# Gated mix of linear attention and a spatial-shift MLP on one core: q tails turned, attention accumulated in w4's banks, VectorE work evened, one early turn and the loads of x, w1 and w2 re-ordered

## The chip, the cores and the metric

The kernel runs on one core of one Trainium2 chip. The metric is the time of one execution on the device, in microseconds; with one core, the slowest core is that core. Each run is put down with its granted TensorE clock and a state: fast, or slow where it lies more than 1.5% above the fastest run of the same kernel. Before the change the median was 259.9 us in 3 runs (259.82 to 260.29).

## The reference

Sequence 2048, width 640, 32 heads of 20, one batch, bf16 inputs. Two blocks read the same x and are mixed by a per-token gate.

```python
def _A_ref(x, wqkv, wo):                       # linear attention
    q, k, v = split_heads(x @ wqkv)            # H = 32, Dh = 20
    phi = lambda t: jnp.where(t > 0, t + 1, jnp.exp(t)) + 1e-6
    pq, pk = phi(q), phi(k)
    kv = einsum("bhsd,bhse->bhde", pk, v)
    z = einsum("bhsd->bhd", pk)
    o = einsum("bhqd,bhde->bhqe", pq, kv) / (einsum("bhqd,bhd->bhq", pq, z)[..., None] + 1e-6)
    return merge_heads(o) @ wo

def _B_ref(x, w1, w2, w3, w4):                 # spatial-shift MLP
    h = _gelu(_layernorm(x) @ w1)
    hs = shift_four_quarters_along_tokens(h) @ w2
    x1 = x + hs
    return x1 + _gelu(_layernorm(x1) @ w3) @ w4     # w3: 640x1728, w4: 1728x640

g = _sigmoid((x * gate_w).sum(-1, keepdims=True))
return g * _A_ref(...) + (1 - g) * _B_ref(...)
```

## The kernel before

The sequence is 16 tiles of 128 tokens, in 4 chunks of 512. A list of work items with dependencies is put in order when the kernel is built, so TensorE's instruction order is fixed. The stages on TensorE are: warm-up, q and k of all tiles with x turned by DMA (to about 53 us); products of phi(k) with x, which stand in for kv because v is never formed (to about 70 us); w1 and w2 (to about 134 us); then w3, attention and w4 mixed together, chunk by chunk, to the end. `phi` is one ScalarE exp and two VectorE operations. TensorE accumulates in 8 banks of 512 fp32 columns; a "held" bank is kept out of the rotation until its owner is done.

The loads of x and of the weights, in the order in which they are issued:

```python
    load_x(4)
    x_turn(3)                                  # a transposing DMA on the SP queue, x_tok -> xT
    # ... gate weights ...
    for c in range(1, NCH):                    # one load for each chunk, then its four turns
        t0 = 5 if c == 1 else 4 * c
        dma_in(x_tok[:, t0:4 * c + 4, :], x2[128 * t0:512 * (c + 1), :].rearrange(...), "xc%d" % c)
        for t in range(4 * c, 4 * c + 4):
            x_turn(t)

    def load_w1():                             # on GpSimd's software queue
        dp = [k_done[5]]
        ...
    def load_w2():
        dp = [k_done[8]]
        ...
```

q of a tile: 5 matmuls of 512 columns and 5 of 128 (the "tail", output columns 512 to 639). The first three tiles are streamed by weight slice, in a hand-written order, where `(2, None)` is the turn of x tile 2 on TensorE and `(t, k)` is slice k of tile t:

```python
    def q_tile(t):
        tok = slice(128 * t, 128 * (t + 1))
        b = pair()
        mm_group(ps[:, b, 0:512], [(xT[:, k, tok], wq[:, k, 0:512]) for k in range(KD)])
        mm_group(ps[:, b + 1, 0:128], [(xT[:, k, tok], wq[:, k, 512:D]) for k in range(KD)])
        phi(b, pq_tok[:, t + 1, :])

    def q_three():
        order = [(0, 0), (1, None), (0, 1), (1, 0), (1, 1), (0, 2), (1, 2), (2, None), (0, 3), (1, 3), (0, 4), (2, 0),
                 (2, 1), (1, 4), (2, 2), (2, 3), (2, 4)]
        stream(order, wq, 128, lambda t, b: phi(b, pq_tok[:, t + 1, :]))
```

Attention of a tile, and its sum into an SBUF accumulator `abx` that already holds (1 - g) * x1. Later w4's result is scaled and added to it:

```python
    def a_tile(t):
        ...
        ts(pool, abx[:, sa, :], x_tok[:, t, :], stg[:, 3, t:t + 1], 0.0, ALU.mult, ALU.add)
        b = pair()
        mm_group(ps[:, b, 0:512], [(pqnT[:, j, tok], M_sb[:, j, 0:512]) for j in range(KD)])
        mm_group(ps[:, b + 1, 0:128], [(pqnT[:, j, tok], M_sb[:, j, 512:D]) for j in range(KD)])
        stt(abx[:, sa, :], psf[:, 512 * b:512 * b + D], stg[:, 2, t:t + 1], abx[:, sa, :], ALU.mult, ALU.add)

    def w4_half(t):                            # first matmuls of a chunk's w4: takes its six banks
        b0, b2, bt = pair(), pair(), pair()
        ...
        bank_hold.update((b0, b0 + 1, b2, b2 + 1, bt, bt + 1))

    def w4_tile(t):
        ...                                    # 13 matmuls, start=False
        for o, n0, n1 in parts:
            stt(x_tok[:, t, n0:n1], o, stg[:, 3, t:t + 1], abx[:, sa, n0:n1], ALU.mult, ALU.add)
```

## Time and profile before

| | before |
|---|---|
| median | 259.9 us (3 runs; 260.04 with three more in the comparison below) |
| span of the profiled run, granted clock | 258.4 us, 1.00 |
| TensorE matmuls, busy | 1600, 255.2 us (99%) |
| start of the first k matmul | 9.91 us |
| start of the first kv product / first attention matmul / last matmul | 53.46 / 138.34 / 256.15 us |

The page of the kernel before, parts 1 (busy time of each engine) and 4 (the chain of work that ended last, by engine):

```profile
PE 255.2 (99%) x1600; PEld 130.5 (51%) x1600; DVE 151.3 (59%) x290; ACT 109.6 (42%) x223; POOL 93.9 (36%) x152
PE 96%; DMA 2%; SPq 0%; DVE 0%; issue 0%
```

TensorE is busy all the time and the chain is nothing but TensorE after the first few microseconds. Such a kernel can be sped up only by fewer or cheaper matmuls, by an earlier start, or by a shorter end after the last matmul (2.29 us here). A busy TensorE is not proof that it issues at its fastest, so the starts of successive matmuls were compared as well: 215.8 ns apart for 512 columns, 109.2 for 256 and 55.8 for 128. The Trainium skill ("TensorE: Matmul & The Clock Gate", the section "Wait — 56ns, not 53.3ns?") gives N / 2.4 GHz plus about 2.5 ns for a warm array. That is 215.8, 109.2 and 55.8 ns, so this trace agrees, and each narrow matmul that is merged away saves 2.5 ns.

The timeline of TensorE at the start of the kernel before (start, duration, engine, source line, operation, and in brackets the idle time before it and what ended it):

```profile
6.74 0.22 PE L899 MATMUL ps<-wq,xT 128*128 128x128 bf16 x1
7.15 0.45 PE L614 MATMUL ps<-ident,x_tok 128*128 128x128 bf16 x5 [0.19 <-DMA x_tok<-in_A_x_dram]
...
9.91 0.38 PE L898 MATMUL ps<-wkg,xT 128*128 128x512 bf16 x1
```

The second line is the turn of x tile 2. It waited 0.19 us for the tile's load, and it is TensorE's last wait for anything but itself.

### The profile page before, as it was taken

The numbers are of one execution on the slowest core, as the hardware profiler recorded it, in microseconds if no ns is written. First come the engines' busy times: TensorE is split into PE (matmuls) and PEld (weight loads), VectorE is DVE, ScalarE is ACT, GpSimd is POOL, SyncE is SP. The second block draws the span as 40 slices with busy tenths as digits, with TensorE's granted clock in tenths as the row PEclk, the third lists the DMA queues.
The fourth block names the chain that finished last, engine by engine and source line by source line (L and its number), as shares of the span: only waits on it lengthen the run. The fifth ranks groups of instructions, "written<-read, shape, count | busy, mean of one in ns | idle before, by whom it ended". The sixth has DMA issues, their size and how long they took to land.

```text
span 258.4 us, 4134 instructions
## 1 busy us (share of the span) xinstructions
PE 255.2 (99%) x1600; PEld 130.5 (51%) x1600; DVE 151.3 (59%) x290; ACT 109.6 (42%) x223; POOL 93.9 (36%) x152
## 2 busy tenths in 40 slices
PE   8999999999999999999999999999999999999996
PEld 3555555544454554555444555444465444644453
DVE  2587877899914999999993403995004410044333
ACT  1496677751366866676854240005510045300000
POOL 5013995969952118767903202222002110012001
PEclk9999999999999999999999999999999999999999
DMA  6764999682764898562825651115010020010211
GB/s 217 215 154 136 208 183 137 178 131 51 100 128 80 152 405 258 65 103 51 105 59 115 123 70 20 28 25 152 0 23 0 0 101 3 0 20 3 103 51 51
DMA packets 54307, 25.86 MB, mean 100 GB/s; under 512 B 45668, under 2 KB 52877, under 8 KB 54288
## 3 DMA queue, kind: packets, MB, share of 16 engines
q1 hardware_dynamic: 52112, 21.21, 37.4%
q0 software_dynamic: 1168, 3.28, 5.7%
q10 hardware_dynamic: 1008, 1.11, 1.2%
q8 instruction: 12, 0.20, 0.3%
q14 instruction: 7, 0.06, 0.1%
HBM read 12.04 MB, written 2.62 MB: 57 GB/s over the span
## 4 chain that ended last, share of the span: by engine, by line
PE 96%; DMA 2%; SPq 0%; DVE 0%; issue 0%
PE ps L603 61%; PE ps L1209 18%; PE ps L805 8%; PE ps L1188 3%; DMA x_tok<-in_A_x_dram 2%; PE ps L898 2%; PE ps L1096 1%; PE ps L1168 1%; SPq L285 0%; PE ps L899 0%; DVE x_tok L642 0%; PE ps L977 0%; PE ps L1006 0%; PE ps L614 0%; PE ps L1172 0%
## 5 line engine op out<-in xcount | busy, mean ns | idle before, releaser
L603 PE MATMUL ps<-xnT,w 128*128 128x512 bf16 x360 | 81.3, 380 | 0.0
L659 ACT ACTIVATE h2T<-ps 128x512 bf16<-128x512 f32 x52 | 30.5, 598 | 60.4 <-PE ps L603 60.4
L603 PEld LDWEIGHTS ps<-xnT,w 128*128 128x128 bf16 x360 | 34.2, 98 | 38.3 <-issue 0.3
L625 POOL TENSOR_SCALAR abx<-x_tok,stg 128x640 f32<-128x640 bf16 x16 | 14.8, 925 | 99.7 <-DVE x_tok L642 94.6
L1209 PE MATMUL ps<-w,h2T 128*128 128x512 bf16 (+1 forms) x260 | 50.1, 348 | 0.0
L642 DVE SCALAR_TENSOR_TENSOR x_tok<-ps,stg,abx 128x512 bf16<-128x512 f32 (+1 forms) x20 | 13.3, 670 | 62.0 <-PE ps L1209 62.0
L625 POOL TENSOR_SCALAR xn<-x_tok,st 128x640 bf16<-128x640 bf16 x32 | 35.3, 1110 | 17.8 <-DMA xnT<-xn 17.3
L1209 PEld LDWEIGHTS ps<-w,h2T 128*128 128x128 bf16 x260 | 22.9, 98 | 22.1 <-issue 0.3
L659 ACT ACTIVATE Er<-ps 128x640 bf16<-128x640 f32 x32 | 22.5, 708 | 15.0 <-PE ps L603 8.0
L658 ACT ACTIVATE junk<-x_tok 128x640 bf16<-128x640 bf16 x32 | 23.6, 739 | 3.4 <-DVE x_tok L640 2.8
L603 PE MATMUL ps<-M_sb,pqnT 128*128 128x512 bf16 (+1 forms) x160 | 24.4, 300 | 0.0
L659 ACT ACTIVATE hsT<-ps 128x512 bf16<-128x512 f32 (+1 forms) x32 | 19.0, 593 | 12.1 <-PE ps L603 11.6
L603 PE MATMUL ps<-w,hsT 128*128 128x512 bf16 (+1 forms) x160 | 23.7, 300 | 0.0
L642 DVE SCALAR_TENSOR_TENSOR abx<-ps,stg,abx 128x640 f32<-128x640 f32 x16 | 14.1, 883 | 15.8 <-PE ps L603 8.8
L603 PE MATMUL ps<-wkg,xT 128*128 128x130 bf16 (+1 forms) x140 | 21.4, 299 | 0.0
L603 PEld LDWEIGHTS ps<-M_sb,pqnT 128*128 128x128 bf16 x160 | 13.6, 98 | 13.0
L603 PE MATMUL ps<-wq,xT 128*128 128x512 bf16 (+1 forms) x130 | 19.8, 300 | 0.0
L603 PEld LDWEIGHTS ps<-w,hsT 128*128 128x128 bf16 x160 | 13.3, 98 | 12.3
L805 PE MATMUL ps<-pk_tok,x_tok 128*128 128x512 bf16 x80 | 17.8, 380 | 0.0
L625 DVE TENSOR_SCALAR Er<-Er 128x640 bf16<-128x640 bf16 x32 | 11.6, 363 | 8.1 <-ACT Er L659 8.0
L1125 DVE TENSOR_TENSOR pq_tok<-pq_tok,dnr 128x300 bf16<-128x300 bf16 (+1 forms) x48 | 15.7, 381 | 0.6
L640 DVE SCALAR_TENSOR_TENSOR x_tok<-ps,x_tok 128x640 bf16<-128x640 f32 x16 | 13.1, 820 | 4.5 <-PE ps L603 3.8
(84 smaller groups left out, 250.6 us busy)
## 6 DMA issues: line engine op xcount, KB each, us to landing
w<-in_B_w_dram SPq DMA_DIRECT2D x1, 2160.0 KB, 8.3
w<-in_B_w_dram SPq DMA_DIRECT2D x1, 2080.0 KB, 13.9
out_dram<-x_tok SPq DMA_DIRECT2D x3, 640.0 KB, 3.1
x_tok<-in_A_x_dram SPq DMA_DIRECT2D x2, 640.0 KB, 5.0
w<-in_B_w_dram POOLq DMA_DIRECT2D x8, 160.0 KB, 4.5
x_tok<-in_A_x_dram SPq DMA_DIRECT2D x5, 160.0 KB, 4.9
wv<-in_A_wqkv_dram POOLq DMA_DIRECT2D x1, 800.0 KB, 6.7
wq<-in_A_wqkv_dram ACTq DMA_DIRECT2D x4, 160.0 KB, 4.1
```

The source lines that it names most:

```text
L603: ins = e.matmul(out_ap, l, r, start=(i == 0), stop=(i == n - 1))
L625: return engf(lambda e: e.tensor_scalar(out_ap, in_ap, s1, s2, op0, op1), rd, [out_ap], cost=cost)
L640: return dve(lambda e: e.scalar_tensor_tensor(out_ap, in0, scalar, in1, op0, op1, accum_out=accum), rd, [out_ap, accum], cost=cost + 70.0)
L642: return dve(lambda e: e.scalar_tensor_tensor(out_ap, in0, scalar, in1, op0, op1), rd, [out_ap], cost=cost)
L658: return act(lambda e: e.activation(out_ap, in_ap, func, bias=bias, scale=scale, accum_out=accum), rd, wr, cost=cost)
L659: return act(lambda e: e.activation(out_ap, in_ap, func, bias=bias, scale=scale), rd, wr, cost=cost)
L805: ins = e.matmul(o, l, r, start=(t0 + q_ == 0), stop=(t0 + q_ == NT - 1))
L898: e.matmul(ps[:, b, 0:512], l, w[:, k, 0:512], start=(k == 0), stop=(k == KD - 1))
L1096: ins = e.matmul(o, l, r, start=st, stop=sp)
L1125: dve(lambda e, o=o, i0=i0, i1=i1: e.tensor_tensor(o, i0, i1, ALU.mult), [i0, dnr[:, 1, sd, :]], [o], cost=cost)
L1188: ins = e.matmul(o, l, r, start=False, stop=(i == KFF - 1))
L1209: ins = e.matmul(o, l, r, start=False, stop=(i == KFF - 1), skip_group_check=(n0 > 0))
```

## The change

Its intent has four parts.

1. **q tails turned.** For tiles 4 to 15 the tails of a chunk's four tiles become one group: the weight slice is the stationary side and 512 tokens stream past. 20 matmuls of 128 columns become 5 of 512. The result is [feature, token], so phi writes it to `mT` and a transposing DMA puts it back.
2. **Attention in w4's banks.** Attention is no longer summed into `abx` by VectorE. Its matmuls open the very banks in which w4 goes on accumulating. For that the attention weights are scaled by g / (1 - g) beforehand, so that the final multiplication by (1 - g) suits both; the gate is made with exp instead of tanh. In chunks 0 to 2 the tails are turned as well (20 narrow matmuls become 10 of 256 columns). In return six banks are held from the attention on, which leaves two for w3.
3. **x tile 2 turned one step later** in the hand-written order.
4. **Loads.** x tiles 8 to 15 come in one load, and w1 and w2 are loaded two and one key tiles later.

The diff, cut to its core:

```diff
-    for c in range(1, NCH):
-        t0 = 5 if c == 1 else 4 * c
-        dma_in(x_tok[:, t0:4 * c + 4, :], ...)
-        for t in range(4 * c, 4 * c + 4):
+    for t0, t1 in ((5, 8), (8, NT)):
+        dma_in(x_tok[:, t0:t1, :], ...)
+        for t in range(4 if t0 == 5 else t0, t1):
             x_turn(t)
     def load_w1():
-        dp = [k_done[5]]
+        dp = [k_done[7]]
     def load_w2():
-        dp = [k_done[8]]
+        dp = [k_done[9]]
@@ q
+    def q_turned(c):
+        b = bank()
+        sl = qx_slot[c] = slot("tl", 2)
+        mm_group(ps[:, b, :], [(wq[:, k, 512:D], xT[:, k, 512 * c:512 * (c + 1)]) for k in range(KD)])
+        phi(b, mT[:, sl, :], n=512)
+    def q_back(c):
+        sch.dma("sp", pq_tok[:, 4 * c + 1:4 * c + 5, 512:D], mT[:, qx_slot[c], :], ..., transpose=True)
     def q_tile(t):
+        if t >= 4:                             # 512 columns only
+            b = bank()
+            mm_group(ps[:, b, :], [(xT[:, k, tok], wq[:, k, 0:512]) for k in range(KD)])
+            phi(b, pq_tok[:, t + 1, 0:512], n=512)
+            return
     def q_three():
-        order = [... (0, 2), (1, 2), (2, None), (0, 3), (1, 3), (0, 4), (2, 0), (2, 1), (1, 4), ...]
+        order = [... (0, 2), (1, 2), (0, 3), (2, None), (1, 3), (0, 4), (1, 4), (2, 0), (2, 1), ...]
@@ gate: exp of the clipped logit; stg[2] = exp(-l), stg[3] = exp(-l) / (1 + exp(-l)) = 1 - g   (cut)
     def qn_scale(t):
-        ts(dve, dnr[:, 0, sd, :], dnr[:, 0, sd, :], EPS_PHI, None, ALU.add, ALU.bypass)
+        ts(dve, dnr[:, 0, sd, :], dnr[:, 0, sd, :], EPS_PHI, stg[:, 2, t:t + 1], ALU.add, ALU.mult)
     def a_tile(t):
-        b = pair()
-        mm_group(ps[:, b, 0:512], ...)
-        mm_group(ps[:, b + 1, 0:128], ...)
-        stt(abx[:, sa, :], psf[...], stg[:, 2, t:t + 1], abx[:, sa, :], ALU.mult, ALU.add)
+        b = w4_banks[t] = bank()
+        bank_hold.add(b)
+        acc([(ps[:, b, :], [(pqnT[:, j, tok], M_sb[:, j, 0:512]) for j in range(KD)])], True)
+        ...                                    # the tails: turned for chunks 0-2, plain for chunk 3
     def w4_half(t):
-        b0, b2, bt = pair(), pair(), pair()
-        ... start=True
+        ... start=False, in the banks that attention opened
```

Cut: moved buffers, item dependencies, GpSimd's share of the gate, and the later start of one statistics chain (the "VectorE work evened").

## The prediction

> **What bounds the kernel now.** TensorE. The page's busy times give PE 255.2 us (99% of a 258.4 us span), DVE 59%, ACT 42%, POOL 36%; the chain of waits is 96% PE; granted clock 1.00. In the timeline PE's last wait is between matmul starts at 6.74 and 7.15 us, for x tile 2's load (0.19 us of it idle). From there to the last matmul at 256.15 us nothing holds it: matmuls start every 215.8 ns (512 columns), 109.2 ns (256) and 55.8 ns (128). The Trainium skill ("TensorE: Matmul & The Clock Gate", the section on 56 ns) states N / 2.4 GHz + 2.5 ns; this trace agrees. The only other losses are 95 ns at each switch to or from half-size matmuls. Some 2.3 us of final VectorE work and store follow. So only fewer columns, fewer matmuls, or the early waits can change the time.
>
> **What the change does.**
> 1. q tails turned (tiles 4-15): per 512 tokens, 20 matmuls of 128 columns (20 x 55.8 = 1.116 us) become 5 of 512 (1.079 us). Columns are equal; 15 fixed costs of 2.5 ns go. Three chunks: 0.11 us.
> 2. Attention accumulated in w4's banks: for chunks 0-2 the 20 narrow matmuls become 10 of 256 columns (1.092 us): 0.075 us in all. The 16 VectorE sums into abx go (0.88 us each, 14.1 us), but VectorE is off the chain: worth nothing. In return six banks are held, leaving w3 two. A w3 group takes 1.08 us; from its last matmul's slot to the end of its gelu (0.60) is 0.80 us in the trace, so two banks should suffice, with 0.2 us to spare.
> 3. x tile 2 turned one step later: a 0.27 us pair of q matmuls moves into the wait before x tile 2. Its weights' last packet ends at 5.33 us, x tile 2's at 6.15 us. Gain 0.27 us. The VectorE copy of tile 2 ends at 8.17 us, needed at about 8.28 us in both.
> 4. VectorE evened: nothing on the chain.
> 5. x tiles 8-15 in one load: at the trace's rate (0.4 MB per us once running) 1.3 MB lands about 24.7 us, tile 8 is turned about 27 us, q tile 8 needs it about 28.9 us. No stall. w1 and w2 load later but are used from 70 us on: worth nothing.
> 6. Gate by exp instead of tanh: off the chain.
>
> **Sum.** 0.11 + 0.075 + 0.27 = 0.46 us, all on the critical path: 259.9 - 0.46 = **259.4 us**, range 258.9 to 260.1 (8 in 10). Chances: faster by over 2% 0.01, within 2% 0.97, slower by over 2% 0.02.
>
> **What the profile should show.** Matmuls 1600 -> 1525; PE still 99%; span about 258.0 us. DVE about 138 us (151.3 - 14.1 + about 1). No PE gap between 7.2 us and the end beyond the 95 ns switches. First k matmul at about 9.64 us (9.91 now); if step 3 fails it stays at 9.91. If step 2's banks fail, w3 groups of chunks 2 and 3 come over 1.08 us apart, waiting for ACT.
>
> **What would make it wrong.** The x load landing after 27 us, so that q tile 8 waits (up to 1 us); the two-bank w3 groups waiting a few tens of ns each (up to 1 us); k, q and the turned tails crowding ACT in the first 50 us (76% busy from 13 to 53 us); a late q tail stalling attention; or a gain in narrow matmuls that I have not seen.

## More of the kernel before

The chain of the kernel before, where the q and k stage ends (start, duration, what):

```profile
47.36 2.72 PE ps L603 x20
50.08 0.27 PE ps L805 x2
50.36 2.72 PE ps L603 x20
53.08 17.00 PE ps L805 x81
```

Each 2.72 us piece is q of one tile and k of another: 20 matmuls, four sorts of five.

The costliest VectorE groups that the change touches, before (line, engine, operation, shapes, count | busy us, mean ns | idle before, releaser):

```profile
L642 DVE SCALAR_TENSOR_TENSOR abx<-ps,stg,abx 128x640 f32<-128x640 f32 x16 | 14.1, 883 | 15.8 <-PE ps L603 8.8 <-POOL abx L625 7.0
L633 DVE TENSOR_TENSOR qprod<-qprod,pk_tok 128x640 f32<-128x640 f32 x13 | 14.0, 1080 | 0.4
L1125 DVE TENSOR_TENSOR pq_tok<-pq_tok,dnr 128x300 bf16<-128x300 bf16 x32 | 13.9, 476 | 0.6
```

The timeline of the SP queue before, from 17 to 44 us: when each x load (L285) and each group of x turns (L281) is issued. A turn is issued only when its load has landed.

```profile
18.74 0.58 SPq L285 DMA_DIRECT2D x_tok<-in_A_x_dram  x1
23.09 5.16 SPq L281 DMA_TRANSPOSE xT<-x_tok  x4
28.30 0.58 SPq L285 DMA_DIRECT2D x_tok<-in_A_x_dram  x1
33.91 5.77 SPq L281 DMA_TRANSPOSE xT<-x_tok  x4
```

x tiles 12 to 15 are asked for at 28.30 us and the turn of tile 12 is issued at 33.91 us. q of tile 12 starts at 41.21 us.

## The result, and the profile after

| | before | changed |
|---|---|---|
| median of 6 runs (lowest to highest) | 260.04 us (259.50 to 260.61) | 259.55 us (259.32 to 259.76) |
| ratio of fast runs, 95% interval | | 0.998 (0.9966 to 0.9995) |
| profiled run | 259.68 us, clock 1.00 | 259.32 us, clock 1.00 |
| matmuls | 1600 | 1525 |
| VectorE busy | 151.3 us | 144.2 us |

A ratio here is the mean time of one kernel's fast runs over that of the other's of the same rounds, so it is not quite the ratio of the medians in the table. By the 2% measure the kernels are the same; the small gain is outside the noise of these runs. It was not seen clear of noise again in the rounds below: e1, e8 and e9 are variants with the same two gains in their traces, and the intervals of their ratios all include 1.

To see where it came from, the TensorE timeline is cut at the same four matmuls in both traces. Each stretch runs from the start of one to the start of the next, us:

| stretch | before | changed | difference |
|---|---|---|---|
| span's start to first k matmul | 9.91 | 9.71 | -0.20 |
| to first kv product (q and k) | 43.55 | 43.44 | -0.11 |
| to first attention matmul | 84.88 | 84.88 | 0 |
| to last matmul | 117.81 | 117.74 | -0.07 |
| tail (VectorE, store) | 2.29 | 2.30 | +0.01 |

Only the second and the fourth difference, 0.18 us together, come back in every trace below that has the same edits and no wait. The first is read from one pair of profiles, and e1, e2 and e8 will show how far it can be trusted.

The page of the changed kernel, the same two parts:

```profile
PE 255.1 (99%) x1525; PEld 128.8 (50%) x1525; DVE 144.2 (56%) x284; ACT 108.5 (42%) x223; POOL 89.3 (35%) x144
PE 97%; DMA 1%; DVE 0%; issue 0%
```

The 75 matmuls that went are 3 x 15 q tails and 3 x 10 attention tails. TensorE's busy time hardly moved, because the columns did not. The start of the changed kernel in TensorE's timeline:

```profile
6.96 0.38 PE L922 MATMUL ps<-wq,xT 128*128 128x512 bf16 x1
7.18 0.22 PE L923 MATMUL ps<-wq,xT 128*128 128x128 bf16 x1
7.23 0.44 PE L614 MATMUL ps<-ident,x_tok 128*128 128x128 bf16 x5
...
9.71 0.38 PE L922 MATMUL ps<-wkg,xT 128*128 128x512 bf16 x1
```

The pair at 6.96 us is the one that moved in front of x tile 2, and the bracket with the wait is gone. TensorE's waits in the whole changed kernel (waited for, us in total, times, longest) confirm that; the one that is left is the very first instruction:

```profile
PE ps L878 <- PEq L1406: 0.8, 1, 0.8
```

The chain of the changed kernel where the q and k stage ends. A q and k piece is now 15 matmuls in 2.44 us, and every fourth is 20 matmuls of the wide sort in 3.52 us, which are one turned group more:

```profile
46.53 2.44 PE ps L603 x15
48.97 0.27 PE ps L805 x2
49.25 3.52 PE ps L603 x20
52.77 17.00 PE ps L805 x81
```

VectorE, the two groups of before that stayed; the sum into abx is gone:

```profile
L633 DVE TENSOR_TENSOR qprod<-qprod,pk_tok 128x640 f32<-128x640 f32 x13 | 16.3, 1251 | 0.5
L1157 DVE TENSOR_TENSOR pq_tok<-pq_tok,dnr 128x300 bf16<-128x300 bf16 x32 | 15.7, 531 | 0.5
```

Both are the same work as before and each is slower by the mean (1080 to 1251 ns, 476 to 531 ns); the last sections come back to that. The SP queue of the changed kernel, 17 to 44 us:

```profile
18.34 0.58 SPq L285 DMA_DIRECT2D x_tok<-in_A_x_dram  x1
25.12 11.06 SPq L281 DMA_TRANSPOSE xT<-x_tok  x8
```

The one load of tiles 8 to 15 is asked for at 18.34 us, its packets run from 19.58 to 24.64 us, and the turn of tile 8 is issued at 25.12 us. q of tile 8 starts at 29.01 us without a wait.

### The profile page after: what moved, and what is told of

The parts are those of the page before. It is cut to its first block, busy times and chain, and to the rows that moved or that the text cites. A ratio compares the mean times of both kernels' runs of the same rounds, so it can differ in the third digit from the quotient of the medians.

```text
span 258.1 us, 3990 instructions
## 1 busy us (share of the span) xinstructions
PE 255.1 (99%) x1525; PEld 128.8 (50%) x1525; DVE 144.2 (56%) x284; ACT 108.5 (42%) x223; POOL 89.3 (35%) x144
## 4 chain that ended last, share of the span: by engine, by line
PE 97%; DMA 1%; DVE 0%; issue 0%
PE ps L603 53%; PE ps L1196 30%; PE ps L805 8%; PE ps L922 2%; DMA x_tok<-in_A_x_dram 1%; PE ps L1128 1%; PE ps L1222 1%; PE ps L923 1%; PE ps L614 0%; DVE x_tok L642 0%; PE ps L1009 0%; PE ps L1038 0%; PE ps L1226 0%; PE ps L878 0%; PE ps L1219 0%
## 5 line engine op out<-in xcount | busy, mean ns | idle before, releaser
L659 ACT ACTIVATE h2T<-ps 128x512 bf16<-128x512 f32 x52 | 30.5, 598 | 62.5 <-PE ps L603 62.5
L625 POOL TENSOR_SCALAR abx<-x_tok,stg 128x640 f32<-128x640 bf16 x16 | 14.0, 879 | 89.4 <-DVE x_tok L642 89.4
L659 ACT ACTIVATE Er<-ps 128x640 bf16<-128x640 f32 (+1 forms) x35 | 22.9, 662 | 15.2 <-PE ps L603 10.0
L1196 PE MATMUL ps<-M_sb,pqnT 128*128 128x512 bf16 (+1 forms) x100 | 21.0, 347 | 0.0
L603 PEld LDWEIGHTS ps<-w,hsT 128*128 128x128 bf16 x160 | 13.3, 98 | 12.3
L1157 DVE TENSOR_TENSOR pq_tok<-pq_tok,dnr 128x300 bf16<-128x300 bf16 (+1 forms) x48 | 17.5, 417 | 0.5
L603 PEld LDWEIGHTS ps<-wkg,xT 128*128 128x128 bf16 x140 | 11.9, 97 | 11.2
L633 DVE TENSOR_TENSOR qprod<-qprod,pk_tok 128x640 f32<-128x640 f32 x13 | 16.3, 1251 | 0.5
L603 PE MATMUL ps<-wq,xT 128*128 128x512 bf16 (+1 forms) x70 | 16.4, 368 | 0.0
L625 DVE TENSOR_SCALAR Er<-Er 128x640 bf16<-128x640 bf16 (+1 forms) x35 | 12.1, 344 | 7.0 <-ACT Er L659 6.4
```

The source lines that it names most:

```text
L603: ins = e.matmul(out_ap, l, r, start=(i == 0), stop=(i == n - 1))
L625: return engf(lambda e: e.tensor_scalar(out_ap, in_ap, s1, s2, op0, op1), rd, [out_ap], cost=cost)
L633: return engf(lambda e: e.tensor_tensor(out_ap, a, b_, op), [a, b_], [out_ap], cost=cost)
L659: return act(lambda e: e.activation(out_ap, in_ap, func, bias=bias, scale=scale), rd, wr, cost=cost)
L1157: dve(lambda e, o=o, i0=i0, i1=i1: e.tensor_tensor(o, i0, i1, ALU.mult), [i0, dnr[:, 1, sd, :]], [o], cost=cost)
L1196: ins = e.matmul(o, l, r, start=first and i == 0, stop=last and i == len(prs) - 1, skip_group_check=True)
```

## The experiments

The theory was that TensorE sets the time, that the three matmul savings add up, and that the rest of the change earns nothing. The rivals: that the start's 0.20 us is chance; that the new load order is what keeps the turned q tails fed; and that VectorE's relief or the free banks are needed by w3. Each kernel ran on a chip together with the kernel before; all results were correct. e1, e2, e3 and e7 shared one chip; e4, e5, e6 and e8 a second; e9 to e12 a third.

In the tables below, "k0" is the start of the first k matmul, "q and k" the stretch from there to the first kv product, and "last stage" that from the first attention matmul to the last matmul, in the profiled run. The stretch between the last two was 84.88 to 84.97 us in every run.

### e1: the old order of the first q matmuls in the changed kernel

```diff
-        order = [... (1, 2), (0, 3), (2, None), (1, 3), (0, 4), (1, 4), (2, 0), (2, 1), ...]
+        order = [... (1, 2), (2, None), (0, 3), (1, 3), (0, 4), (2, 0), (2, 1), (1, 4), ...]
```

> The changed kernel with step 3 alone undone (x tile 2 is turned where it was before). Theory (TensorE columns plus the start): a PE gap of about 0.1 to 0.36 us in front of the turn of x tile 2 comes back, the first k matmul starts at about 9.9 us instead of 9.71, and from there to the last matmul the trace is as in the changed kernel (246.06 us): about 0.2 us slower than the changed kernel, about 0.2 us faster than before (ratio 0.999). Rival (the gain is VectorE's relief: 14 us of sums gone): the time stays at the changed kernel's, ratio to before 0.998, and the first k matmul does not matter.

### e2: the new order alone, in the kernel before

The reverse of e1's edit, in the kernel before.

> The kernel before with step 3 alone. Theory: the first k matmul starts 0.2 to 0.27 us earlier than before's 9.91 us, the stretch from it to the last matmul stays 246.24 us as before, time about 0.2 us less than before (ratio 0.999). Rival (VectorE's relief): no change at all, since VectorE does the same work.

| | k0 | q and k | last stage | median (6 runs) | ratio to before (95%) |
|---|---|---|---|---|---|
| e1 | 9.89 | 43.43 | 117.74 | 260.70 | 1.0011 (0.9987 to 1.0036) |
| e2 | 9.50 | 43.55 | 117.81 | 259.64 | 0.9998 (0.9975 to 1.0022) |

The stretches behave as they should: e1 has the q and k stretch and the last stage of the changed kernel, e2 those of the kernel before. The times do not decide about the order, for neither interval excludes 1. The start of e1 in TensorE's timeline shows why one look is not enough:

```profile
7.09 0.22 PE L923 MATMUL ps<-wq,xT 128*128 128x128 bf16 x1
7.15 0.33 PE L614 MATMUL ps<-ident,x_tok 128*128 128x128 bf16 x3
```

The old order had no wait in front of the turn in this run. TensorE itself was later there: its matmuls ran at half pace until 5.6 us, against 3.6 us in the profile of the kernel before. The start is set by whichever comes last, the clock's ramp or an arrival, and both move from run to run.

### e8: a longer warm-up in the changed kernel

```diff
-    WARM = 3456
+    WARM = 3712
```

> The changed kernel with a longer warm-up (3712 columns where it was 3456: 0.21 us more of made-up matmuls, in the gap of 0.3 us before the first turn of x). In the profile of the changed kernel matmuls ran at half pace until 5.1 us, in that of before until 3.6 us, so the start is open to chance. Theory: it fills an idle stretch and changes nothing else; if it makes the full clock come earlier, the first real q product starts by 4.55 us and the time is 0 to 0.2 us less than the changed kernel's; else it is the same, or up to 0.1 us more.

k0 was 9.70 us, q and k 43.43, last stage 117.74; the median 259.63 us, ratio 0.9994 (0.9964 to 1.0024). The half pace lasted to 5.16 us as in the changed kernel (5.17). In this one profile 256 columns more of warm-up did not move the start; beside the scatter that follows, a small effect would not show.

The 14 profiles, taken together, show what does. Up to the first k matmul there are 6.49 us of matmuls, counted at full pace, after 0.83 us of waiting for the first one (6.60 us in e8). To that come what half pace adds, roughly 1.3 to 2.9 us, and waits for arrivals, roughly 0.1 to 1.6 us, of which the largest was a piece of wq (0.78 to 0.83 us between matmul starts above a matmul's time, in three profiles) and the next x tile 2 (0.23 to 0.51 us, in six). So k0 lies anywhere from 9.50 to 10.92 us: from 9.50 to 9.91 us in seven profiles and from 10.38 us on in the other seven. In front of the turn of x tile 2, the old order waited in three of its four profiles (0.36, 0, 0.32 and 0.31 us), the new one in five of its ten (0.43, 0.23, 0.51, 0.12 and 0.09 us). The means differ by 0.11 us. That speaks for a gain of about 0.1 us, from few profiles, beside a scatter of 1.4 us in the start, of which each order alone shows more than 1 us.

### e3: the turned q tails alone, in the kernel before

```diff
+    def q_turned(c): ...                       # as in the change, with phi's width and the buffers
+    def q_back(c): ...
     def q_tile(t):
+        if t >= 4:
+            ...                                # 512 columns only
             addA(("q", i), ...)
+            if i >= 4 and i % 4 == 3:
+                addA(("qx", i // 4), 1.08, lambda c=i // 4: q_turned(c))
+                IT.add("QB", ("qb", i // 4), 0.0, lambda c=i // 4: q_back(c), ...)
```

> The kernel before with the turned q tails alone (with the small moves of memory that they need). Theory: the stretch from the first k matmul to the first product of the G accumulation after the last k tile shrinks by 0.11 us, nothing after it changes, matmuls 1600 to 1555, first k matmul at 9.9 us; time about 0.1 us less than before, too little for the timing to show (ratio 0.9996). If narrow matmuls cost more than their 55.8 ns slots, the stretch shrinks by more. A late tail from the second transposition would show as a PE wait in the attention products after 138 us.

k0 10.92, q and k 45.73, last stage 117.82, 1555 matmuls; the median 260.85 us, ratio 1.0044 (1.0008 to 1.0080). The tails were worth 0.11 us in the changed kernel. Alone they cost 2.2 us in the profiled run (45.73 against 43.55), which is the slowest of the six (259.52 to 262.99 us). The reason is mainly one line in TensorE's timeline:

```profile
44.44 1.25 PE L603 MATMUL ps<-wq,xT 128*128 128x512 bf16 x5 [1.94 <-DMA xT<-x_tok]
```

q of tile 12 waited for the turned x tile 12. This run had the old loads. So the prediction's "worth nothing" for the loads was in doubt, and e5 took it up.

### e5: the old loads in the changed kernel

```diff
-    for t0, t1 in ((5, 8), (8, NT)):           # one load for tiles 8-15
+    for c in range(1, NCH):                    # one load per chunk
     def load_w1():
-        dp = [k_done[7]]
+        dp = [k_done[5]]
     def load_w2():
-        dp = [k_done[9]]
+        dp = [k_done[8]]
```

> The changed kernel with the loads as they were (x tiles 8-11 and 12-15 apart, w1 after key tile 5, w2 after key tile 8). PE's order is the same instruction for instruction. Theory: no PE wait between 7.3 us and the end in either, time as the changed kernel (259.55 us). Rival: the q and k stage, now 0.27 us shorter per step, outruns the old loads, and q tiles 12-15 wait for x, by 0.2 to 2 us between 40 and 50 us.

TensorE's instruction order is the same as in the changed kernel. The six runs were 270.42 (slow, clock 0.987), 259.60, 265.26 (slow, 0.994), 263.74 (slow, 0.993), 260.44 and 259.76 us. The ratio of the three fast ones is 0.9996 (0.9961 to 1.0031). The profiled run is the slowest, and its TensorE waits are:

```profile
PE ps L603 <- DMA xT<-x_tok: 7.1, 2, 4.1
```

Its SP queue:

```profile
29.08 0.58 SPq L285 DMA_DIRECT2D x_tok<-in_A_x_dram  x1
41.40 5.16 SPq L281 DMA_TRANSPOSE xT<-x_tok  x4
```

The load of tiles 12 to 15 was asked for at 29.08 us and the first turn was issued at 41.40 us: 12.3 us, against 5.6 us (28.30 to 33.91) in the kernel before. TensorE stood still for tile 12 (3.19 us between matmul starts) and for tile 15 (4.22 us). The late turn of tile 15 fell on the next software load, that of wv: the turn's packets ran from 49.38 to 54.62 us. After each stop it ran at half pace for about 3.5 us (45.5 to 49 and 59 to 62.5 us). The q and k stretch is 54.40 us, 10.97 us longer than in the changed kernel: 7.41 us of waits and 3.5 us for twice 3.5 us at half pace. The low clock follows the waits in time, and 7 us at half pace in a span of 269 us make the 0.987. So the "slow" label of this run is a result of the waits and not a disturbance from outside (the two other slow runs have no trace); e3, whose runs were all fast, shows the same wait.

The packets explain the delay. The load shares the SP queue with the turns. Its packets ran from 34.29 to 40.29 us, and began only as those of the turns of tiles 10 and 11 ended, at 32.3 and 34.7 us; and w1's packets on the software queue had been under way beside them since 26.56 us. This agrees with the Trainium skill ("DMA: Bandwidth & Descriptors", the section "Queues, rings and completion order"): a DMA engine takes its descriptors in ring order within a queue and goes round between queues packet by packet, so a second queue slows the first and a load cannot pass the turns ahead of it.

### e9, e10 and e12: which part of the loads matters

e9 is the changed kernel with the old x loads and the late w1 and w2. e10 is the changed kernel with the one x load and the early w1 and w2. e12 is the kernel before with both new parts.

```diff
# e9, in the changed kernel
-    for t0, t1 in ((5, 8), (8, NT)):           # one load for tiles 8-15
+    for c in range(1, NCH):                    # one load per chunk
# e10, in the changed kernel
-        dp = [k_done[7]]                       # w1
+        dp = [k_done[5]]
-        dp = [k_done[9]]                       # w2
+        dp = [k_done[8]]
# e12, in the kernel before
-    for c in range(1, NCH):                    # one load per chunk
+    for t0, t1 in ((5, 8), (8, NT)):           # one load for tiles 8-15
-        dp = [k_done[5]]                       # w1
+        dp = [k_done[7]]
-        dp = [k_done[8]]                       # w2
+        dp = [k_done[9]]
```

> The changed kernel with x tiles 8-15 in two loads as before; w1 and w2 stay late. PE's order is unchanged. Theory A (in the runs that stalled, the load of x tiles 12-15 stood in its queue behind the turns of tiles 10 and 11, which w1's packets had slowed): with w1 not yet started at 29 us that load lands by about 33.5 us, tile 12 is turned by 37 us, needed at 39.6; no PE wait between 8 and 53 us in the profile, all runs at 259.3 to 261 us. Theory B (a second load of x is late by itself): PE waits again near 40 us, by 1 us or more, and some runs are over 262 us.

> The changed kernel with one load of x tiles 8-15, but w1 after key tile 5 and w2 after key tile 8 as before. PE's order is unchanged. Theory A: the whole of x is in by 25 us, before w1 starts at about 26.6 us, so no load queues behind slowed turns; the turns of tiles 10-15 get slower (last packet of tile 12 after 33 us) but are needed only from 34 us (tile 10) to 49 us (tile 15): no PE wait, or under 1 us. Theory C (w1's packets by themselves slow the turns too much, so only the later w1 helps): PE waits for a turned tile between 34 and 50 us by over 1 us, some runs are over 262 us.

> The kernel before with the new loads alone. Theory: in before's profile nothing on PE waits for a turned tile (tile 12's last packet at 36.8 us, needed at 41.2), so the new loads leave the stretch from the first k matmul to the last product of the k and q stage at 43.55 us and the time at 260.0 us. Rival (the new loads alone give the gain, because before too lost time to late turns in its slower runs): the times lie at 259.3 to 259.8 us with no run over 260.2, ratio 0.998.

| | k0 | q and k | last stage | median (6 runs) | ratio to before (95%) |
|---|---|---|---|---|---|
| e9 | 10.44 | 43.43 | 117.74 | 259.89 | 0.9977 (0.9947 to 1.0006) |
| e10 | 10.38 | 44.74 | 117.74 | 261.46 | 1.0037 (1.0003 to 1.0071) |
| e12 | 10.52 | 43.55 | 117.82 | 259.97 | 0.9990 (0.9956 to 1.0024) |

(The traces of e9 to e12 lack 27 to 29 matmul records; a gap as long as one missing matmul is not counted as a wait.) In e9 no wait is left between 13 and 60 us, and none of its six runs is over 260.64 us, where three of e5's six were over 263. Its SP queue shows the load of tiles 12 to 15, asked for at almost the same time as in e5, with its last packet at 33.34 us and turned from 33.77 us:

```profile
29.19 0.58 SPq L285 DMA_DIRECT2D x_tok<-in_A_x_dram  x1
33.77 6.29 SPq L281 DMA_TRANSPOSE xT<-x_tok  x4
```

So the later w1 and w2 suffice by themselves. e10 shows that the single load does not. Its waits, if any, were expected at tiles 10 to 15; the main one came earlier, at tile 8, in TensorE's timeline:

```profile
30.97 1.25 PE L603 MATMUL ps<-wq,xT 128*128 128x512 bf16 x5 [0.81 <-DMA xT<-x_tok]
```

The turn of tile 8 was issued at 25.91 us and its packets took from 27.09 to 29.12 us, 2.03 us where in the changed kernel it takes 0.94, while w1's load was under way (from 27.66 us). The wait is 0.97 us between matmul starts. The other 0.31 us of e10's longer stretch is a wait for tile 4 at 17.5 us, before any of these loads; e7 has one at the same tile. The single load puts tile 8's turn 2 us later than the split one would, and then the early w1 falls on it. In e12 the loads changed nothing: 43.55 us, as in the kernel before. The later w1 and w2 are a precondition of the turned tails, not a gain; the single x load is not even needed.

### e7: the changed kernel without the turned q tails

```diff
-    def q_turned(c): ...
-    def q_back(c): ...
     def q_tile(t):
-        if t >= 4:
-            ...                                # 512 columns only
         ...                                    # 640 columns for every tile
-            if i >= 4 and i % 4 == 3: ...      # the items qx, qb and what waits for qb
```

> The changed kernel with the turned q tails alone undone (attention in w4's banks, the new start and the new loads stay). Theory: matmuls 1570; the q and k stage is 0.11 us longer than in the changed kernel, the stretch from the end of the G accumulation to the last matmul stays as in the changed kernel, 0.075 us shorter than before; VectorE busy about 144 us, 7 us less than before, without any further gain in time. Time 259.65 us, ratio to before about 0.9985. Rival (VectorE's relief): all of the 0.49 us stays, ratio 0.998, and PE's stretch after 138 us would be shorter by more than 0.1 us.

k0 10.59, q and k 43.77 (43.55 and a wait of 0.21 for tile 4), last stage 117.74; 1570 matmuls; VectorE busy 141.0 us. The median was 260.44 us, ratio 1.0014 (0.9994 to 1.0034). The stretches are what the sum says: without the tails q and k are back at the old value once the wait is taken off, and attention keeps its own 0.07 us. The total drowns in the start, which was among the seven late ones.

### e4 and e11: VectorE loaded again

A useless VectorE operation of the size of the removed sum follows each attention tile in the changed kernel, twice in e4 and once in e11. It writes a scratch buffer, so the result stays right.

```diff
         acc([(ps[:, b, :], [(pqnT[:, j, tok], M_sb[:, j, 0:512]) for j in range(KD)])], True)
+        for _ in range(2):                    # e11: once
+            stt(qprod[:, :], x_tok[:, t, :], stg[:, 3, t:t + 1], x_tok[:, t, :], ALU.mult, ALU.add)
```

> The changed kernel with two made-up VectorE sums of 128x640 into scratch after each attention tile: 32 more instructions of roughly 0.8 us each (about 26 us, more than the 14 us that the change took away), result unchanged. Theory: VectorE busy 144 to about 170 us, PE matmuls start at the same times, last matmul at 255.8 us, ratio of time to the changed kernel 1.000. Rival (VectorE's relief is what pays): time goes back to before's 260.0 us or above it, with PE waiting for VectorE in the w4 stages.

> The changed kernel with one made-up VectorE sum per attention tile: 16 x about 0.88 us, the 14 us that the change took away. PE's order is unchanged. First theory (on record before the experiments: VectorE is off the chain, its relief worth nothing): no change, ratio to the changed kernel 1.000. Revised theory (after the run with twice as much): w3's third chunk has only the two banks that VectorE frees last; with this load the second of them comes free after it is needed (173.5 us), one w3 group waits 0.85 us, time 260.4 us: the relief is what makes the held banks free of cost, without gaining anything by itself.

| | VectorE busy | q and k | last stage | median (6 runs) | ratio to before (95%) |
|---|---|---|---|---|---|
| changed | 144.2 | 43.44 | 117.74 | 259.55 | 0.9980 (0.9966 to 0.9995) |
| e11, one per tile | 157.1 | 43.44 | 118.60 | 261.16 | 1.0023 (0.9991 to 1.0054) |
| e4, two per tile | 174.0 | 43.44 | 119.47 | 261.09 | 1.0044 (1.0020 to 1.0068) |

With one operation per tile, the last stage is 0.86 us longer, and with two 1.72 us. These are one and two waits in front of w3 groups of chunk 2. That of e11, in TensorE's timeline:

```profile
173.29 1.24 PE L603 MATMUL ps<-xnT,w 128*128 128x512 bf16 x5
175.23 5.14 PE L603 MATMUL ps<-xnT,w 128*128 128x512 bf16 x22 [0.69 <-ACT h2T L659]
```

The bracket shows 0.69 us idle; between matmul starts it is 0.852 us, because the modelled end of a matmul lies 0.16 us after the next could start. The changed kernel has no wait there. What came late is a bank. Two are left to w3 at this place: that of w4's tile 2 of the chunk before, and that of tile 3, which VectorE has to evacuate first. Which group gets which is settled when the kernel is built, by when each is reckoned to come free. The built kernels say: in the changed kernel the first two groups of chunk 2 get tile 2's bank and tile 3's; in e11, with VectorE reckoned to be later, both get tile 2's, so that the second waits for the first one's gelu, which is the ACT in the bracket. VectorE's timeline has that evacuation at

```profile
171.10 0.74 DVE L642 SCALAR_TENSOR_TENSOR x_tok<-ps,stg,abx 128x512 bf16<-128x512 f32 x1
```

in the changed kernel, at

```profile
173.48 0.75 DVE L642 SCALAR_TENSOR_TENSOR x_tok<-ps,stg,abx 128x512 bf16<-128x512 f32 x1
```

in the kernel before, and at

```profile
174.58 0.75 DVE L642 SCALAR_TENSOR_TENSOR x_tok<-ps,stg,abx 128x512 bf16<-128x512 f32 x1
```

in e11. The second w3 group of chunk 2 is due 1.08 us after the first has started, so at 173.5 us in the changed kernel and at 174.4 us in e11. In the changed kernel tile 3's bank is free by 171.84 us. In e11 it is free only after 175.3 us, so that waiting for it instead would have saved nothing. In the kernel before, an evacuation until 174.2 us did no harm, because attention held no banks there. So without the removal of the sums the new bank layout would have cost about 0.86 us, more than the whole change brings. That the removal earns nothing on its own is argued, not run: in the kernel before, TensorE waited for nothing in this stage. Between matmuls this is exact; the total times of e4 and e11 also contain the start (9.73 and 10.59 us in the profiled runs) and were taken on different chips, so they do not rank the two.

### e6: one bank for w3

```diff
     def w3_group(c, j):
+        if c == 2 and j == 0:                 # take a bank out of the rotation for chunk 2
+            spare.append(bank())
+            bank_pend.discard(spare[0])
+            bank_hold.add(spare[0])
         ...
+        if c == 2 and j == KFF - 1:
+            bank_hold.discard(spare[0])
```

> The changed kernel with one more bank held during w3's third chunk, so that its 13 groups share one bank where they had two. PE's order is the same. Theory: from a group's last matmul slot to the end of its gelu is 0.80 us, and PE has to wait for it: 12 times about 0.85 to 1.0 us, so 10 to 12 us longer, all between 173 and 200 us; the two other w3 chunks stay at 1.08 us per group. That shows the margin by which two banks suffice. Rival (banks do not matter here, ACT would keep up): no change.

One run: 270.54 us, last stage 128.09 us, 10.35 us more than the changed kernel. TensorE's timeline:

```profile
175.17 1.25 PE L603 MATMUL ps<-xnT,w 128*128 128x512 bf16 x5 [0.69 <-ACT h2T L659]
177.11 1.25 PE L603 MATMUL ps<-xnT,w 128*128 128x512 bf16 x5 [0.69 <-ACT h2T L659]
```

Twelve groups waited 0.852 us each (10.2 us), so that they start 1.94 us apart instead of 1.08. The Trainium skill ("Perfetto Trace Analysis", the section "Optimizing Tensor Performance") says that independent groups should rotate through different banks so that one's evacuation overlaps the next one's matmuls. The trace agrees and gives the size: with two banks a gelu may take up to a whole group's 1.08 us, and it needs 0.80 us of it; with one, TensorE stands for all of that time and 0.05 us more.

## Why the prediction was right or wrong, point by point

**The whole.** 259.4 us was predicted with 258.9 to 260.1; 259.55 us was measured. "Within 2%" was right. That the median came so close is partly luck: of the 0.49 us between the two medians, 0.18 us lies in stretches that every trace confirms, and the rest lies in the start, which scatters by 1.4 us from run to run.

**TensorE bounds the kernel: right, and shown.** Every experiment that left TensorE without a wait had the same stretches to 0.02 us: 43.43 to 43.44 us for q and k with the tails turned, 43.55 us without, 117.74 against 117.81 or 117.82 us for the last stage.

**Step 1, q tails, 0.11 us: right.** 43.55 to 43.44 us. e7 takes it away again. But e3 shows that it holds only where the x tiles come in time.

**Step 2, attention in w4's banks, 0.075 us: right in size.** 117.81 to 117.74 us, and two banks suffice for w3, as the 0.80 of 1.08 us had said. Of the removed sums the prediction said that "VectorE is off the chain: worth nothing". Nothing contradicts that for the sums alone, but without VectorE's relief w3's second bank does not come free in time (e11: 0.86 us). The argument looked at VectorE's place on the chain of the kernel before; the change moved the chain's slack.

**Step 3, x tile 2 later, 0.27 us: not shown, and probably smaller.** The one pair of profiles gives 0.20 us, and the first k matmul stood at 9.71 us where 9.64 was named. The wait that went was only 0.19 us of idle (0.41 us between starts); a whole pair of matmuls of 0.27 us fitted in front of it. But the start scatters by 1.4 us between runs, the two profiles of the pair left half pace at different times (3.56 and 5.17 us), neither e1 nor e2 shows the step in time, and e1's profile has no wait with the old order. The 14 profiles together speak for about 0.1 us; the step is likely and is not shown.

**Step 5, loads: wrong in "worth nothing".** The landing of the single load was right (24.7 us predicted; last packet at 24.64 us, turn issued at 25.12 us), as was "no stall". The failed step is "w1 and w2 load later but are used from 70 us on: worth nothing". It asked when w1 and w2 are needed and not what their packets get in the way of. With the old loads and the turned tails, TensorE waits 2.1 us (e3) or 7.4 us between starts (e5) for turned x tiles; with only w1 and w2 late, it does not (e9). The total was still right because the loads were part of the change, and because the old kernel does not suffer from its old loads (e12).

**What stays open.** Why the kernel before hardly ever waits with the old loads was not isolated. Its w1 starts at 27.22 us, 0.7 us later than in e5, and falls one turn later in the chain of turns; that is argued only. What the traces do show is that the turns of tiles 10 and 11 were over at 30.0 us there and at 34.7 us in e5, with w1's packets beside them in both. Nor is it known why half of e5's runs escape the wait.

**VectorE's busy time: 138 us predicted, 144.2 us measured.** The sums into abx (14.1 us) did go. The failed term is "about 1" for what comes in. The transposed phi takes 2.1 us, against 1.6 us saved in the ordinary one, and the gate and the scaling of the denominator take 1.5 us. Most of the rest is old work that got slower: 2.2 us in the z sums and 1.7 us in the products with the reciprocal. (Together these make 5.9 us of the 7.0; the remainder was not traced.) For the z sums the trace suggests a reason. In the kernel before, VectorE's groups in two windows, first 55.0 to 60.9 us and then 64.6 to 70.2 us:

```profile
L633 DVE TENSOR_TENSOR qprod<-qprod,pk_tok 128x640 f32<-128x640 f32 x6 | 5.0, 828 | 0.2
```

```profile
L633 DVE TENSOR_TENSOR qprod<-qprod,pk_tok 128x640 f32<-128x640 f32 x4 | 5.5, 1384 | 0.1
```

The same instruction takes 828 or 1384 ns. In the first window GpSimd works on 4-column statistics; in the second it normalizes x tiles. In the changed kernel GpSimd begins these normalizations at 56.45 us instead of 60.98 us, and so 10 of the 13 sums are slow (1307 to 1386 ns) instead of 6. Four more at 0.56 us make the 2.2 us. The Trainium skill ("SBUF — State Buffer", the section "Who interferes with whom") says that a VectorE instruction with two SBUF inputs contends with a GpSimd instruction that reads SBUF. Both inputs of the z sum are in SBUF, and these instructions agree with it. No run took GpSimd's work away to test it, and for the products the cause was not looked into. None of this cost time, because TensorE waited for none of it.

**Step 4 and 6** were put at nothing, and no stretch shows anything of them by themselves.

**A better version?** None was found. e9 has the lowest ratio after the changed kernel, and the same stretches (43.43 against 43.44 us), so the two are alike.

## What to carry to other kernels

When one engine is busy for 99% of the time, cost a change in that engine's own terms (here columns and 2.5 ns per matmul); it came out to a hundredth of a microsecond. But ask of every part that is "off the chain" what it frees and what it gets in the way of: a VectorE sum was worth nothing until six banks were held, and a load that was wanted only some 40 us later (w1, asked for from 27 us and used from 70 us) could cost the turns beside it several microseconds. And do not judge a 0.2 us step at the start of a kernel from one pair of profiles when the start itself scatters by 1.4 us: compare stretches between fixed instructions instead of totals.

## What the Trainium skill lacked or had wrong

- "TensorE: Matmul & The Clock Gate", "Part 1: The HAM clock gate": the page puts the change to full pace at about 4 us of matmul activity, give or take 500 ns. In 14 profiles the first matmul started at 0.83 us and the last at half pace between 3.56 and 6.60 us, a spread of 3.0 us; its note that the number of slow matmuls varies fits better than the 500 ns.
- "Perfetto Trace Analysis", "Optimizing Tensor Performance": it says to rotate banks, with no size. Here a second bank was worth 0.852 us for each group of 1.08 us (e6).
- "DMA: Bandwidth & Descriptors": no page has a time for an on-chip transposing DMA of 128 x 640 beside a load on another queue. Here the turn of tile 8 took 0.94 us of packets alone and 2.03 us beside w1's load (changed kernel, e10). A load of 640 KB behind such turns took 6.0 us of packets in e5 and 2.9 us without w1 beside it in e9, but also only 3.1 us in the kernel before, where w1 was under way; so the price varies.
- "SBUF — State Buffer", "Who interferes with whom": the page has the contention of VectorE with GpSimd for an instruction with two SBUF inputs, but no size for it (the full blocking that it names is for VectorE's 2-port modes). In the kernel before the sums took 1384 ns instead of 828 ns beside normalizations of 1432 ns (64.6 to 70.2 us), so one pair every 1.43 us; the fastest normalizations take about 870 ns, and one after the other the pair would take 1.70 us (an estimate from these two). So, if this contention is the cause, less than the whole of each was blocked.
- No page has the scatter of the first arrivals: TensorE waited up to 0.83 us for a piece of wq in three of the 14 profiles and up to 0.51 us for x tile 2 in six, in kernels whose early loads are the same.
